# Moving reciprocals, seeds and a transpose in the attention stage of a fused attention and SoLU kernel

## The chip, the cores and the metric

The kernel runs on one core of a Trainium2 chip. The metric is the device time of one execution in microseconds; the figure for a kernel is the median of its runs. Five engines work side by side, each through its own instructions in the order in which the program gives them: PE (TensorE, the matmuls), DVE (VectorE), ACT (ScalarE), POOL (GpSimd) and SP (SyncE, which here issues nearly all DMAs). They wait for one another and for DMAs through semaphores.

## The reference

The kernel computes attention with normalised queries and keys, and feeds its output into a feed-forward block.

```python
# q, k, v: (8, 12, 448, 64)
q_n, k_n = rmsnorm(q, g_q), rmsnorm(k, g_k)     # x / sqrt(mean(x*x) + 1e-6) * g
attn = softmax(q_n @ k_n.T / 8)                 # rows of 448
x = (attn @ v), heads side by side              # (3584, 768)
h = x @ w_in                                    # (3584, 1024)
solu = h * softmax(h)
ln = (solu - mean) / sqrt(var + 1e-6) * g_ln
out = ln @ w_out                                # (3584, 768)
```

The softmax of the attention is not divided out where it is computed. The exponentials go into the value product as they are; their row sums are computed beside, are inverted, and are multiplied in later, when `x` is read for the product with `w_in`.

## The kernel before, in words

All of the work lies in `fast_path`. It has three stages one after the other: attention, the product with `w_in` with the SoLU and its normalisation, and the product with `w_out`. Both products are by a scheme with seven block products in place of eight. The order of the instructions is written out by hand (`tc.manual_schedule()`), so the order of the lines in the loop is the order on each engine.

**Attention by quads.** The 96 pairs of batch and head are taken four at a time, which makes 24 quads (`NQ`). The loop over `m` from 1 to 23 does one quad in each turn. A turn works on several quads at once:

- PE computes the scores of quad `m` in seven pieces of 64 keys (`both_scores`, L885) and the products with the values (`both_values`, L897). ACT takes the exponential of each piece (`exponentials`, L845). The output of the values lies in one PSUM buffer, `o`, of which there is one only: before PE may begin the values of quad `m`, DVE must have copied out the quad before (`take(m - 1)`, L1000, `xo<-o`).
- DVE adds up the exponentials of the quad so that the row sums need fewer matmuls: `add_pair` (L905), `add_to` (L911) and, for the quads in the table `two_terms`, `join_terms` (L915), which adds the two partial sums `es` into one. What is left are the quad's terms: the exponentials `El` of the last piece, and one or two `es`. After each quad in `sums_at` (2, 5, 8, 11, ..., 23) PE sums the terms of the quads since the last such place with matmuls against ones (`sums`, L962, eight matmul records for each term), ACT copies the result (L974), and SP sends it to DRAM (`sd`, L979).
- For quad `m + 1`, POOL scales queries and keys by their inverse norms (`normalise`, L735, `qkn`), DVE transposes the two halves (`qk_transpose`, L756, `qkT`), and ACT multiplies the gain in (`gains`, L751). The scores of quad `m + 1` wait for that.
- For quad `m + 2` the norms are prepared: ACT squares (L690), DVE sums rows (`row_sums`, L696), POOL folds the sums (`fold_sums`, L706 and L707), ACT makes a first guess of the inverse root by a logarithm and an exponential (`rsqrt_seed`, L713 and L714) and, if told to, its square (L717). At the start of the next turn DVE improves the guess (`rsqrt_step`): where the square is there by L724 and L729, otherwise by L727, L728 and L729.
- For 12 turns (`steps_at`) ACT and DVE also convert a piece of `w_in` (L538, L539 on ACT, L545 and L546 on DVE), and POOL combines blocks of `w_in` (`combine_in`, L567) after a gate (L570).

**The inverses.** The table `inverts_at` says in which turn the row sums of a batch are inverted: turns 4, 8, 10, 14, 16, 20 and 22. At the start of such a turn SP loads them from DRAM (`load_sums`, L988, `inv<-sd`). At the end of the turn, behind the additions and before `take(m)` of the next turn, DVE takes the reciprocal (`invert`, L992). In the turn after, SP writes them back (`send_inverses`, L995).

**SP's queue.** In each turn SP issues, in this order: the values of quad `m + 1` (`load_v`, L675), the output of the last quad (`store_x`, L1009, which waits for `take(m - 1)`), the sums and inverses if there are any (L979, L995, L988), a piece of `w_in` (L513), and eight to ten pieces of queries and keys of a later quad (L647). One instruction that waits holds up all that stand behind it.

Of the kernel before, what the change touches and what calls it, by code (L numbers as in the profile page):

```python
# [366 lines left out]
def fast_path(  # L367
# [24 lines left out]
    nc = tc.nc  # L392
# [294 lines left out]
    def squares(n):  # L687
        d = st[n]
        d["sq"] = work.tile([P, 2 * NB, 32], FP32, tag="sq", name="sq", bufs=2)
        nc.scalar.activation(d["sq"].rearrange("p (s b) d -> p s (b d)", s=2), d["qk"], AF.Square)  # L690

    def row_sums(n):
        m, i = divmod(n, 2)
        if i == 0:
            norms[m] = {"part": work.tile([P, 2, 2 * NB], FP32, tag="part", name="part", bufs=2)}
        nc.vector.tensor_reduce(norms[m]["part"][:, i], st[n]["sq"], AX, OP.add)  # L696
# [12 lines left out]
    def rsqrt_seed(d, square=False):  # L709
        ss = d["ss"]  # L710
        p, w = ss.shape
        y = d["y"] = work.tile([P, 4 * NB], FP32, tag="ny", name="ny", bufs=2)[0:p, 0:w]
        nc.scalar.activation(y, ss, AF.Ln, scale=1.0 / D, bias=eps[0:p])  # L713
        nc.scalar.activation(y, y, AF.Exp, scale=-0.5)  # L714
        if square:
            x = d["x"] = work.tile([P, 4 * NB], FP32, tag="nx", name="nx", bufs=2)[0:p, 0:w]
            nc.scalar.activation(x, y, AF.Square)  # L717
# [35 lines left out]
    def qk_transpose(n):  # L753
        d = st[n]
        turned(n)
        nc.vector.transpose(d["qkT"].rearrange("p s t -> p (s t)"), d["qkn"].rearrange("p b d -> p (b d)"))  # L756
# [709 lines left out]
    combines_at = {11 + 3 * (x // 2) + x % 2: (x,) for x in range(8)}  # L1466
    combines_at[22] = (8,)
    combines_at[23] = (10, 11)
    two_terms = (3, 4, 6, 7, 9, 10, 12, 13, 15, 16, 18, 19, 21, 22, 23)
    sums_at = (2, 5) + tuple(range(8, NQ, 3))  # L1470
    inverts_at = {4: (0,), 8: (1,), 10: (2,), 14: (3,), 16: (4,), 20: (5,), 22: (6,)}
    wq += [(moe_w_out, c + k, i) for c in range(HF) for k in (0, HF) for i in range(2)]
# [31 lines left out]
    with tc.manual_schedule():  # L1504
# [68 lines left out]
        for m in range(1, NQ):  # L1573
            a, b = 2 * m, 2 * m + 1
            next1 = m + 1 < NQ
            next2 = m + 2 < NQ
            early = EARLY <= m
            four = m < 3

            def score(x):  # L1580
                unit(lambda: both_scores(m, x))

            def value(x):
                unit(lambda: both_values(m, x))

            if m == 3:
                norm_gain()
            sent = None
            if kept:
                sent = keep_sums(*kept)  # L1590
                kept = None
            if next1:
                load_v(m + 1)
            beside = combines_at.get(m, ())
            if beside:
                if m - 1 in steps_at:
                    step = wq[steps_at.index(m - 1)]
                    pass_on(w_in[(0, 3, 1, 2)[step[1] // HD * 2 + step[2]]][0:1, step[1] % HD, 0:1])
                else:
                    pass_on(quads[m - 1]["terms"][-1][1][0:1, 0, 0:1])  # L1600
                for x in beside:
                    combine_in(x)
                take(m - 1)
            if early and next1:
                rsqrt_step(norms[m + 1])
            if m > 1 and not beside:
                take(m - 1)
            store_x(m - 1)
            if sent:
                sent()  # L1610
            for x in inverts_at.get(m - 1, ()):
                send_inverses(x)
            for x in inverts_at.get(m, ()):
                load_sums(x)
            if early and m + 2 in steps_at:
                load_next()
            if m == 1:
                score(0)
                score(1)
                score(2)  # L1620
                rsqrt_seed(norms[2])
                rsqrt_step(norms[2])
                normalise(4)
                normalise(5)
                load_pieces(8)
                score(3)
                squares(6)
                row_sums(6)
                qk_transpose(4)
                value(0)  # L1630
                score(4)
                squares(7)
                row_sums(7)
                qk_transpose(5)
                value(1)
                score(5)
                fold_sums(3)
                value(2)
                score(6)
                gains(2)  # L1640
                rsqrt_seed(norms[3])
                add_pair(m, 0, 1)
                add_to(m, 0, 2, nc.vector)
            else:
                if next1:
                    if not early:
                        rsqrt_step(norms[m + 1])
                    if m == 2:
                        add_pair(1, 3, 4)
                        quads[1]["terms"].append((2, quads[1]["E", 5]))  # L1650
                    normalise(a + 2)
                    normalise(b + 2)
                    if m == 22:
                        combine_in(9)
                if early:
                    load_pieces(2)
                else:
                    load_pieces(10)
                    if m + 2 in steps_at:
                        load_next()  # L1660
                if early and next2:
                    row_sums(a + 4)
                    row_sums(b + 4)
                    load_pieces(6)
                if m == NQ - 1:
                    scale(0)
                score(0)
                if m > 2 and not early:
                    squares(a + 4)
                    row_sums(a + 4)  # L1670
                score(1)
                if next1:
                    qk_transpose(a + 2)
                if m > 2 and not early:
                    squares(b + 4)
                    row_sums(b + 4)
                if m == 2:
                    score(2)
                    squares(a + 4)
                    row_sums(a + 4)  # L1680
                    score(3)
                    squares(b + 4)
                    row_sums(b + 4)
                    qk_transpose(b + 2)
                else:
                    if next1:
                        qk_transpose(b + 2)
                    score(2)
                    score(3)
                if next2:  # L1690
                    fold_sums(m + 2)
                value(0)
                score(4)
                if m in steps_at:
                    low_bits, join, product = convert_w(wq[steps_at.index(m)], raws[steps_at.index(m)])
                    low_bits[0]()
                value(1)
                score(5)
                if m in steps_at:
                    low_bits[1]()  # L1700
                if next1 and early and m not in sums_at:
                    gains(m + 1)
                add_pair(m, 0, 1)
                if four:
                    add_to(m, 0, 2, nc.vector)
                    add_pair(m, 3, 4)
                else:
                    add_pair(m, 2, 3)
                    add_to(m, 0, 4, nc.vector)
                    add_to(m, 1, 5, nc.vector)  # L1710
                    if m in two_terms:
                        join_terms(m)
                value(2)
                score(6)
                if next1 and (not early or m in sums_at):
                    gains(m + 1)
                if m in steps_at:
                    join()
                if next2:
                    rsqrt_seed(norms[m + 2], True)  # L1720
                if m + 1 >= EARLY and m + 3 < NQ:
                    squares(a + 6)
                    squares(b + 6)
                if four:
                    quads[m]["terms"].append((2, quads[m]["E", 5]))
            quads[m]["terms"].insert(0, (2, quads[m]["E", NK - 1]))
            if m == NQ - 2:
                load_x(0)
                load_r(0)
            if m == NQ - 1:  # L1730
                load_x(1)
                sizes(0)
                block_sums(0, 0)
                block_sums(0, 1)
            for x in inverts_at.get(m, ()):
                invert(x)
            for x in range(3, NK):
                value(x)
            waiting.append(m)
            if m in sums_at:  # L1740
                unit(lambda: None)
                kept = end_sums()
                waiting.clear()
# [188 lines left out]
```

## Time and profile before

| what | value |
|---|---|
| median of 3 runs | 780.86 us (780.45 to 781.51) |
| the profiled execution's own time | 782.57 us |
| its span from first to last instruction | 780.8 us |
| PE busy | 767.3 us (98%) |
| DVE busy | 612.4 us (78%) |
| ACT busy | 514.1 us (66%) |
| POOL busy | 486.6 us (62%) |

The page gives the busy time of each engine, in forty slices of the span too, the chain of work that ended last, and groups of instructions by line. Attention takes the stretch up to about 298.7 us, where the first matmul with `w_in` (L1114) begins; from 548.7 us on the last of these are under way, and the products with `w_out` (L1340) follow. A row of the timeline gives start, duration, engine, line, operation, what is written from what is read, and how often; in square brackets stands how long the engine was idle ahead of it, and who ended that.

### The profile page before, as it was taken

What the parts mean: (1) busy time and instruction counts of PE and PEld (TensorE: products, weight loads), DVE (VectorE), ACT (ScalarE), POOL (GpSimd) and SP (SyncE); (2) the same over time, 40 slices, a digit from 0 to 9 for tenths busy, and PEclk for the clock granted to TensorE, in tenths of its full rate; (3) what the DMA queues carried; (4) which work ended last, traced back from release to release, by engine and by line L of the source; (5) the groups of instructions that cost most, each with busy time, mean ns of one, the idle gap of its engine ahead of it and who ended that gap; (6) DMA issues with size and microseconds to landing.
All of it is one profiled execution on the core that took longest, in us unless ns stands there. A gap on an engine that the chain in (4) does not pass through costs nothing.

```text
span 780.8 us, 14823 instructions
## 1 busy us (share of the span) xinstructions
PE 767.3 (98%) x5142; PEld 473.8 (61%) x5142; DVE 612.4 (78%) x1034; ACT 514.1 (66%) x853; POOL 486.6 (62%) x635
## 2 busy tenths in 40 slices
PE   8999999999999999999999999999999999999996
PEld 4444444444444444444444444444899999999996
DVE  6779999999999984687878766685797685776844
ACT  6688898988989862787777756655626445464410
POOL 2554543455464452455677688888898787777852
PEclk9999999999999999999999999999999999999999
DMA  9999999999999376588887767773756647446212
GB/s 159 169 188 178 206 166 201 200 189 182 209 196 183 104 180 143 142 197 182 199 187 179 165 148 166 166 179 70 224 157 232 209 143 256 155 176 247 98 62 86
DMA packets 279817, 134.26 MB, mean 172 GB/s; under 512 B 190324, under 2 KB 264884, under 8 KB 279732
## 3 DMA queue, kind: packets, MB, share of 16 engines
q1 hardware_dynamic: 265892, 123.31, 70.5%
q10 hardware_dynamic: 13840, 9.90, 4.3%
q8 instruction: 43, 0.70, 0.4%
q14 instruction: 42, 0.34, 0.1%
HBM read 96.12 MB, written 37.04 MB: 171 GB/s over the span
## 4 chain that ended last, share of the span: by engine, by line
PE 83%; SPq 6%; DVE 4%; DMA 3%; issue 2%; POOL 2%; ACT 1%; DVEq 0%; POOLq 0%; ACTq 0%
PE A L1340 16%; PE A L1114 14%; PE s L885 10%; PE o L897 10%; PE B L1114 9%; PE B L1340 8%; PE D L1114 5%; PE C L1114 5%; SPq L647 4%; PE C L1340 4%; PE sm L962 2%; POOL qkn L735 1%; DMA qk<-in_q_dram 1%; DVE es L911 1%; DMA qk<-in_k_dram 1%
## 5 line engine op out<-in xcount | busy, mean ns | idle before, releaser
L885 PE MATMUL s<-qkT 64*64 64x448 f32 x1288 | 140.5, 542 | 1.1 <-ACT qkT L751 1.0
L845 ACT ACTIVATE E<-s 128x896 f32<-128x896 f32 x144 | 124.4, 920 | 18.5 <-PE s L885 17.8
L897 PE MATMUL o<-E,v 64*64 64x448 f32 x1104 | 120.8, 537 | 1.6 <-DVE xo L1000 1.1
L735 POOL TENSOR_TENSOR qkn<-qk,ny 128x896 f32<-128x896 f32 x45 | 77.2, 1736 | 67.7 <-DVE ny L729 32.4
L885 PEld LDWEIGHTS s<-qkT 64*64 64x64 f32 x1288 | 66.2, 191 | 61.9 <-issue 37.9
L1340 PE MATMUL A<-w_out,sums 128*128 128x192 f32 x392 | 79.7, 326 | 0.0
L1340 PE MATMUL B<-w_out,sums 128*128 128x192 f32 x392 | 79.7, 326 | 0.0
L897 PEld LDWEIGHTS o<-E,v 64*64 64x64 f32 x1104 | 42.0, 133 | 58.9 <-issue 47.9
L1114 PE MATMUL A<-w_in,xg 128*128 128x512 f32 x168 | 76.8, 593 | 0.0
L1114 PE MATMUL B<-w_in,xsum 128*128 128x512 f32 x168 | 76.7, 592 | 0.0
L1340 PEld LDWEIGHTS A<-w_out,sums 128*128 128x128 f32 x392 | 66.3, 190 | 0.0
L1340 PEld LDWEIGHTS B<-w_out,sums 128*128 128x128 f32 x392 | 66.3, 190 | 0.0
L756 DVE STREAM_TRANSPOSE qkT<-qkn 128x896 f32<-128x896 f32 x46 | 50.0, 1099 | 9.7 <-POOL qkn L735 9.7
L1114 PEld LDWEIGHTS B<-w_in,xsum 128*128 128x128 f32 x168 | 31.9, 190 | 40.2 <-issue 39.9
L1114 PEld LDWEIGHTS A<-w_in,xg 128*128 128x128 f32 x168 | 31.8, 190 | 40.1 <-issue 38.9
L1216 ACT ACTIVATE u<-u,shift,he 128x1024 f32<-128x1024 f32 x28 | 34.8, 1242 | 28.7 <-POOL shift L1212 28.6
L696 DVE TENSOR_REDUCE part<-sq 128x28 f32<-128x896 f32 x46 | 47.9, 1075 | 6.3 <-ACT sq L690 6.3
L1090 POOL TENSOR_TENSOR xsum<-xg 128x384 f32<-128x384 f32 x14 | 14.4, 1032 | 57.9 <-ACT xsum L1073 45.1
L905 DVE TENSOR_TENSOR es<-E 128x896 f32<-128x896 f32 x46 | 49.4, 1110 | 0.0
L911 DVE TENSOR_TENSOR es<-es,E 128x896 f32<-128x896 f32 x44 | 47.9, 1126 | 0.1
L1340 PE MATMUL A<-w_out,s 128*128 128x192 f32 x224 | 45.5, 326 | 0.0
L690 ACT ACTIVATE sq<-qk 128x896 f32<-128x896 f32 x45 | 41.0, 945 | 3.2 <-DMA qk<-in_k_dram 2.4
(175 smaller groups left out, 1660.7 us busy)
## 6 DMA issues: line engine op xcount, KB each, us to landing
ur<-ud SPq DMA_DIRECT2D x60, 256.0 KB, 4.6
ud<-ub SPq DMA_DIRECT2D x112, 128.0 KB, 2.9
xd<-xo SPq DMA_DIRECT2D x48, 224.0 KB, 4.1
qk<-in_q_dram SPq DMA_DIRECT2D x92, 112.0 KB, 4.5
qk<-in_k_dram SPq DMA_DIRECT2D x92, 112.0 KB, 4.2
v<-in_v_dram SPq DMA_DIRECT2D x23, 448.0 KB, 3.9
out_dram<-P SPq DMA_DIRECT2D x19, 384.0 KB, 4.0
raw<-in_moe_w_in_dram SPq DMA_DIRECT2D x12, 512.0 KB, 5.7
```

Of the source, the lines that this page charges most:

```text
L690: nc.scalar.activation(d["sq"].rearrange("p (s b) d -> p s (b d)", s=2), d["qk"], AF.Square)
L696: nc.vector.tensor_reduce(norms[m]["part"][:, i], st[n]["sq"], AX, OP.add)
L735: e.tensor_tensor(d["qkn"].rearrange("p (s b) d -> p s b d", s=2), d["qk"].rearrange("p s (b d) -> p s b d", d=32), y.rearrange("p (s b) - ...
L756: nc.vector.transpose(d["qkT"].rearrange("p s t -> p (s t)"), d["qkn"].rearrange("p b d -> p (b d)"))
L845: nc.scalar.activation(e, s[:, :, 0:S], AF.Exp)
L885: nc.tensor.matmul(s[i * D : (i + 1) * D, h, 0:S], qkT[hh, i, 1, keys], qkT[hh, i, 0], start=True, stop=True)
L897: nc.tensor.matmul(d["o"][h * D : (h + 1) * D, i, 0:S], d["v"][pp, h, kc], d["E", kc][pp, h], start=kc == 0, stop=kc == NK - 1,)
L905: nc.vector.tensor_tensor(e, d["E", x], d["E", y], OP.add)
L911: engine.tensor_tensor(e, e, d["E", x], OP.add)
L1114: nc.tensor.matmul(k[bank], a[:, c], w_in[i][:, c], start=begin and c == 0, stop=c == HD - 1, skip_group_check=not begin,)
L1216: nc.scalar.activation(d["u"], d["u"], AF.Identity, scale=d["e"], bias=d["shift"])
L1340: nc.tensor.matmul(k[bank], a[:, c].rearrange("p a i -> p (a i)"), w_out[:, area, i, c], start=begin and c == 0, stop=c == KC - 1, skip_gr ...
```

## The change

The change makes five edits, all in the loop over the quads, and no other function is touched.

1. `invert(x)` moves, for the turns from 4 on, from the end of the turn to the place right behind the second `qk_transpose`, ahead of the additions. `load_sums` and `send_inverses` stay where they are.
2. In turn 1 the second transpose comes ahead of `row_sums(7)`; the seed for quad 3 and two additions of quad 1 move from the end of turn 1 into turn 2. There the additions are first, then `score(0)`, then the seed.
3. Quads 21 and 23 leave the table `two_terms`: they keep two `es` and El, three terms.
4. The square of the seed by ACT is left out in turns 6, 9, 12, 15, 18 and 21; in the turn that follows, DVE does `rsqrt_step` with three instructions in place of two.
5. The first entry of a quad's terms is put in with `setdefault`, since quad 1 has no terms yet at that place.

```diff
-    two_terms = (3, 4, 6, 7, 9, 10, 12, 13, 15, 16, 18, 19, 21, 22, 23)
+    two_terms = (3, 4, 6, 7, 9, 10, 12, 13, 15, 16, 18, 19, 22)
...
+                qk_transpose(5)
                 row_sums(7)
-                qk_transpose(5)
...
-                rsqrt_seed(norms[3])
-                add_pair(m, 0, 1)
-                add_to(m, 0, 2, nc.vector)
             else:
+                if m == 2:
+                    add_pair(1, 0, 1)
+                    add_to(1, 1, 2, nc.vector)
+                    score(0)
+                    rsqrt_seed(norms[3])
...
-                score(0)
+                if m != 2:
+                    score(0)
...
                     if next1:
                         qk_transpose(b + 2)
+                    for x in inverts_at.get(m, ()):
+                        invert(x)
                     score(2)
                     score(3)
...
-                    rsqrt_seed(norms[m + 2], True)
+                    rsqrt_seed(norms[m + 2], m not in steps_at or m + 1 in steps_at)
...
-            quads[m]["terms"].insert(0, (2, quads[m]["E", NK - 1]))
+            quads[m].setdefault("terms", []).insert(0, (2, quads[m]["E", NK - 1]))
...
-            for x in inverts_at.get(m, ()):
-                invert(x)
```

On DVE the rows of turn 8 show the first edit (`qkT` is the transposed queries and keys, `inv` the row sums to be inverted, `es` the added exponentials, `w_in_90` a block of weights):

```order
 L696 TENSOR_REDUCE part<-sq 128x28 x2
 L756 STREAM_TRANSPOSE qkT<-qkn 128x896 x2
+L992 RECIPROCAL inv<-inv 128x42
 L905 TENSOR_TENSOR es<-E 128x896 x2
 L911 TENSOR_TENSOR es<-es,E 128x896 x2
 L545 SCALAR_TENSOR_TENSOR tmp<-raw,tmp 128x512
 L546 SCALAR_TENSOR_TENSOR w_in_90<-raw,tmp 128x512
-L992 RECIPROCAL inv<-inv 128x42
```

The reciprocal moved ahead of four additions and of the two steps of a weight's conversion; nothing else in the turn moved.

On DVE the rows from the end of turn 1 into turn 2 show the second edit (`part` are the row sums of squares, `xo` the copy of a quad's output):

```order
 L696 TENSOR_REDUCE part<-sq 128x28
-L756 STREAM_TRANSPOSE qkT<-qkn 128x896
+L756 STREAM_TRANSPOSE qkT<-qkn 128x896 x2
 L696 TENSOR_REDUCE part<-sq 128x28
-L756 STREAM_TRANSPOSE qkT<-qkn 128x896
+L1000 COPY xo<-o 128x896
 L905 TENSOR_TENSOR es<-E 128x896
 L911 TENSOR_TENSOR es<-es,E 128x896
-L1000 COPY xo<-o 128x896
```

The second transpose moved one place up, ahead of the row sums, and the copy of the output moved ahead of two additions.

On PE the rows at the end of attention show the third edit (`sm` are the row sums in PSUM, `El` the exponentials of the last piece, four matmuls of the program for each term, in the order of quads 21, 22 and 23):

```order
 L962 MATMUL sm<-El,ones 32x224 x4
+L962 MATMUL sm<-es,ones 32x224 x8
+L962 MATMUL sm<-El,ones 32x224 x4
 L962 MATMUL sm<-es,ones 32x224 x4
 L962 MATMUL sm<-El,ones 32x224 x4
-L962 MATMUL sm<-es,ones 32x224 x4
-L962 MATMUL sm<-El,ones 32x224 x4
-L962 MATMUL sm<-es,ones 32x224 x4
+L962 MATMUL sm<-es,ones 32x224 x8
 L1114 MATMUL A<-w_in_88,xg 128x512 x3
```

There are two more groups of four matmuls with `es`: one for quad 21 and one for quad 23, the latter last of all.

## Prediction

> **What bounds the kernel now.** I read the page first, then PE's waits, then busy times by stage, then the timelines of DVE, PE and SP at the places where the change acts.
>
> ```profile
> PE 767.3 (98%) x5142; PEld 473.8 (61%) x5142; DVE 612.4 (78%) x1034; ACT 514.1 (66%) x853; POOL 486.6 (62%) x635
> ```
>
> PE is the engine that sets the time: from the first scores to the last product it hardly rests. So an edit gains only where PE waits today, and costs only where it makes PE wait. PE's waits that the change can touch:
>
> ```profile
> PE sm L962 <- DVE es L915: 1.4, 1, 1.4
> PE o L897 <- DVE xo L1000: 1.1, 2, 0.6
> PE s L885 <- ACT qkT L751: 1.0, 1, 1.0
> ```
>
> These are 3.5 us in all. More telling are the busy times in attention (columns: stretch, its length, busy time and instructions of PE, PEld, DVE, ACT, POOL, then clock, DMA share, GB/s):
>
> ```profile
> 80.00:120.00 40.00, 40.00 (x456) 18.83 (x452) 39.72 (x48) 36.40 (x55) 17.19 (x27) 1.00 0.98 188
> 160.00:200.00 40.00, 40.00 (x452) 19.36 (x448) 38.38 (x45) 36.03 (x52) 20.84 (x31) 1.00 1.02 200
> ```
>
> PE is full, but DVE is too, at 96 to 99%, and so are the DMA engines, with a share of about 1. The 78% of DVE on the page is a mean over three stages and hides that. DVE has no lead over PE either, at the end of attention (DVE's copy of quad 21's output; PE's first value product of quads 22 and 23):
>
> ```profile
> 274.02 1.08 DVE L1000 COPY xo<-o 128x896 f32<-128x896 f32 x1
> ```
>
> ```profile
> 275.15 0.98 PE L897 MATMUL o<-E,v 64*64 64x448 f32 x8
> 286.96 0.98 PE L897 MATMUL o<-E,v 64*64 64x448 f32 x8 [0.57 <-DVE xo L1000]
> ```
>
> The copy ends at 275.10 and PE begins 0.05 us later; one quad on, PE waits 0.57. So whatever DVE loses anywhere in attention has become PE's loss by quad 23. That is the reading on which the rest hangs.
>
> **The reciprocals (edit 1).** The instruction costs the same at either place. What counts is when its input lands. In turn 8 DVE does this:
>
> ```profile
> 113.22 2.10 DVE L756 STREAM_TRANSPOSE qkT<-qkn 128x896 f32<-128x896 f32 x2
> 115.23 2.05 DVE L905 TENSOR_TENSOR es<-E 128x896 f32<-128x896 f32 x2
> 117.20 2.09 DVE L911 TENSOR_TENSOR es<-es,E 128x896 f32<-128x896 f32 x2
> 119.93 0.69 DVE L546 SCALAR_TENSOR_TENSOR w_in<-raw,tmp 128x512 uint32<-128x512 uint32 x1
> 120.99 0.42 DVE L992 RECIPROCAL inv<-inv 128x42 f32<-128x42 f32 x1 [0.37 <-DMA qk<-in_q_dram]
> 121.33 0.15 DVE L724 SCALAR_TENSOR_TENSOR nx<-ss,nx 128x56 f32<-128x56 f32 x1
> ```
>
> SP issued the load here:
>
> ```profile
> 115.80 1.23 SPq L1009 DMA_DIRECT2D xd<-xo  x2
> 117.09 0.84 SPq L988 DMA_DIRECT2D inv<-sd  x1
> ```
>
> The reciprocal waited even at its late place: 0.37 us, for a DMA. Its input landed at 120.99, 3.9 us after the issue. In the new place DVE comes to it at 115.23, when the load is not yet issued, and stands for 5.8 us. Behind it on DVE are the four additions, the two weight steps, the norm's step and the copy `xo`; for these wait PE's sums, POOL's `qkn`, PE's values and SP's store. The additions begin at 121.33 instead of 115.23, 6.10 later. From the step of the norm on (121.33 before) the delay is 6.10 less what is vacated between 120.62, when L546 ends, and 121.33: 5.39.
>
> PE feels it first at the sums of turn 8, whose last two terms are this quad's `es`:
>
> ```profile
> 121.33 0.94 PE L962 MATMUL sm<-es,ones 128*32 128x224 f32 x16
> ```
>
> The last addition ends 6.10 after 119.29 (117.20, where L911 starts, and its 2.09), at 125.4. PE begins the second of the two terms 0.38 us (the step between two terms, below) behind 121.33, at 121.7, so it loses 3.7 there; the rest of the 5.39 comes as DVE's lead goes over the next quads.
>
> Would the early gain of edit 2 (below, 1.0) be kept? Only as far as SP comes earlier, since the landing sets the time here. SP goes from one issue to the next (117.03, 117.09) on DMA engines that are full, so it can hardly come earlier by all of that; I count about two thirds, 0.65, as earlier landing: 5.39 - 0.65 = 4.74.
>
> For the other turns SP's lag no longer holds: when DVE is 5 us later, SP has caught up and is held by the copy `xo` itself. Turn 4 shows that spacing (DVE's copy, then SP), and a tile's answer for turn 16 the landing:
>
> ```profile
> 63.97 1.08 DVE L1000 COPY xo<-o 128x896 f32<-128x896 f32 x1
> ...
> 69.24 1.10 DVE L756 STREAM_TRANSPOSE qkT<-qkn 128x896 f32<-128x896 f32 x1
> ```
>
> ```profile
> 65.08 1.26 SPq L1009 DMA_DIRECT2D xd<-xo  x2
> 66.40 1.58 SPq L988 DMA_DIRECT2D inv<-sd  x1
> ```
>
> ```profile
> DMA to landing us min/median/max: 3.5/3.5/3.5
> ```
>
> So the inverse lands 1.35 + 3.5 = 4.85 us after the copy ends. Turns 10 and 14 show how long DVE takes from the copy's end to the end of the transposes:
>
> ```profile
> 133.46 1.08 DVE L1000 COPY xo<-o 128x896 f32<-128x896 f32 x1
> 136.45 2.10 DVE L756 STREAM_TRANSPOSE qkT<-qkn 128x896 f32<-128x896 f32 x2
> ```
>
> ```profile
> 178.78 1.08 DVE L1000 COPY xo<-o 128x896 f32<-128x896 f32 x1
> 184.14 1.11 DVE L756 STREAM_TRANSPOSE qkT<-qkn 128x896 f32<-128x896 f32 x1 [0.46 <-POOL qkn L735]
> ```
>
> That is 4.0 us in turn 10, where the norm's step comes ahead of the copy, 5.4 in turn 14 and 5.3 in turn 4. Turn 16 has the order of turn 10, turns 20 and 22 that of 14. I count 1.0 each for turns 10 and 16, and nothing for 4, 14, 20 and 22, where the transposes cover the load by about 0.5. If SP still lagged in 14 and 20, each would add up to about 1; that goes into the range.
>
> [...]
>
> **The squares (edit 4).**
>
> ```profile
> L717 ACT ACTIVATE nx<-ny x20: 249/249/251, 49.6 to 271.6; 128x56 f32<-128x56 f32 x20
> L728 DVE TENSOR_TENSOR nx<-nx,ny x5: 174/216/218, 6.9 to 39.5; 128x56 f32<-128x56 f32 x3, 112x16 f32<-112x16 f32 x2
> ```
>
> ACT sheds six of these, 1.5 us, and it is nobody's bound there. DVE gains six at 0.22. The one in turn 7 is swallowed by the wait in turn 8; the other five add 1.1 to a full engine. In turns 10, 13, 16 and 19 it stands ahead of the copy, in turn 22 ahead of POOL's `qkn`.
>
> **Three terms (edit 3).** The join of quad 21 takes 1.09 us of DVE, just ahead of quad 22's copy: -1.09. At the end of attention (DVE's adds and join of quad 23; PE's sums):
>
> ```profile
> 271.68 1.09 DVE L915 TENSOR_TENSOR es<-es 128x896 f32<-128x896 f32 x1
> ```
>
> ```profile
> 292.62 3.70 DVE L911 TENSOR_TENSOR es<-es,E 128x896 f32<-128x896 f32 x2
> 296.35 1.77 DVE L915 TENSOR_TENSOR es<-es 128x896 f32<-128x896 f32 x1
> ```
>
> ```profile
> 295.80 0.56 PE L962 MATMUL sm<-es,ones 128*32 128x224 f32 x8
> 296.18 0.56 PE L962 MATMUL sm<-El,ones 128*32 128x224 f32 x8
> 298.18 0.59 PE L962 MATMUL sm<-es,ones 128*32 128x224 f32 x8 [1.44 <-DVE es L915]
> ```
>
> Without the join, quad 23's second `es` is ready at 296.32 instead of 298.12. PE spends 0.38 us on a term (295.80 to 296.18) and has two more, 0.76; it comes to the last one later than 296.32 and doesn't wait. So the end gets 1.44 - 0.76 = 0.68 shorter.
>
> **The third quad (edit 2).** PE waits ahead of the scores of quad 2:
>
> ```profile
> 37.35 3.69 PE L885 MATMUL s<-qkT 64*64 64x448 f32 x32 [0.96 <-ACT qkT L751]
> ```
>
> ```profile
> 34.16 1.04 DVE L696 TENSOR_REDUCE part<-sq 128x28 f32<-128x896 f32 x1
> 35.12 1.10 DVE L756 STREAM_TRANSPOSE qkT<-qkn 128x896 f32<-128x896 f32 x1
> ```
>
> With the row sums behind the transpose, that ends 0.96 earlier, and the 0.96 goes. The seed then waits for a POOL that gets its sums about 1 us later, but stands behind the first exponential and no longer holds it. I take the gain as 1.0, with 0 and 1.4 as its bounds; the wait in turn 8 swallows most of it in any case, as counted above. Edit 5 moves nothing.
>
> **The sum.** DVE at quad 22's copy: 4.74 + 2.0 (turns 10, 16) + 1.1 (steps) - 1.09 (join) = 6.75 later. The end: 6.75 - 0.68 = 6.1. The two later stages are PE without a gap, and shift as a whole. The profiled execution took 782.57 us, with its span of 780.8 inside; the median is 780.86, 1.7 below it. Forecast: 782.57 + 6.1 = 788.7 for that execution, 787.0 for the median.
>
> Its own bounds: 785.3 if SP comes earlier by the whole early gain and turns 10 and 16 cost half; 789.7 if SP comes no earlier and turns 14 and 20 cost 1 each.
>
> PE will stand still for some 3.7 us in turn 8, longer than any wait of before after its start. [...]
>
> **The rivals.**
>
> *The inverses are there in time: faster.* If SP came 5.8 us earlier in turn 8, or at any rate ahead of the transposes, no reciprocal would wait. Then the gains stand alone: 0.96 at quad 2, 0.57 at quad 23's copy (the join of quad 21 gives DVE 1.09, the added steps take 1.1, the start gives 0.96) and 0.68 at the end, 2.2 in all: 778.6. It decides at a landing before 115.23. For it: the load's time hangs on a DMA backlog that another order can shift. Against it: 5.8 us is half a turn, and compute that comes 1 us earlier makes SP's lag larger, not smaller. Chance 0.08.
>
> *SP stays behind in every turn.* If the lag is fixed against DVE and not against the clock, each turn pays its own. The load of turn 10:
>
> ```profile
> 139.51 0.73 SPq L988 DMA_DIRECT2D inv<-sd  x1
> ```
>
> With 3.5 to 3.9 us to landing, turn 10 would wait from 138.5 until about 143.2, 4.7 us. If turns 14, 16 and 20 are no better, that is 18.8 in place of 2.0: up to 804. Against it: SP gets 5 us of rest in which the DMAs drain. Chance 0.07.
>
> *The wait is absorbed.* DVE's delay of turn 8 could be made up if it has more lead than the rows show, or the load may land so much sooner that only 1 to 2 us are left against the gains: 780 to 782. The two rows leave DVE 0.3 and 1.6 us in 40, and those rests are waits for POOL such as the 0.46 in turn 14, which come along. Chance 0.08 for within 0.2%.
>
> **How the numbers follow.** The forecast has 0.76. It and the second rival are slower: 0.83; faster 0.09, same 0.08 (0.2% is 1.6 us, about what a measurement of this kernel can tell from none). The range, 782.3 to 792.5, takes the forecast's own bounds, reaches down to the absorbed wait and up to one or two turns that wait as the second rival has it.
>
> **What would show it.** Right: in turn 8 DVE idle for 5 to 6 us ahead of L992, ended by a DMA; a wait of PE of 3 to 4 us for `es` at the sums of turn 8; about 1 us ahead of L992 in turns 10 and 16; no wait ahead of the last sums; the first L1114 at about 304.8 instead of 298.7. Wrong: L992 without a wait in turn 8, or the first L1114 below 299.

## The result and the profile after

The changed kernel takes 790.94 us (median of 4 runs, 790.05 to 792.71), the kernel before, run beside it, 781.00: a ratio of 1.013, with an interval of 1.0111 to 1.0149. The change costs 9.9 us; 787.0 was forecast. The profiled execution took 791.04 us with a span of 789.4, so the two spans differ by 8.6. The rest of the 9.9 comes from the two profiled executions: that of before (782.57 us) was itself longer than its median, that of after was not.

The page's first line, then two of PE's waits:

```profile
PE 769.7 (97%) x5158; PEld 473.1 (60%) x5158; DVE 610.2 (77%) x1038; ACT 511.8 (65%) x847; POOL 483.3 (61%) x635
```

```profile
PE o L897 <- DVE xo L1000: 6.4, 8, 1.5
PE sm L962 <- DVE es L911: 2.9, 5, 1.2
```

PE's waits for DVE's copy `xo` went from 1.1 to 6.4 us, and a wait for the additions is new. DVE's waits name the place:

```profile
DVE inv L992 <- DMA inv<-sd: 8.6, 5, 3.7
```

The reciprocal stands for its load in five turns, 8.6 us in all; before, that was 0.37. The busy times by stage show whom it costs (columns as in the prediction):

```profile
80.00:120.00 40.00, 40.00 (x468) 18.94 (x464) 36.05 (x45) 36.44 (x53) 16.50 (x26) 1.00 1.05 191
...
160.00:200.00 40.00, 38.08 (x428) 17.82 (x424) 36.88 (x45) 33.67 (x49) 19.25 (x27) 1.00 0.98 179
```

In the stretch up to 120 us DVE now rests (36.05 us busy instead of 39.72), and in the later stretch PE does (38.08 instead of 40.00). The clock column stays at 1.00. Turn 8 on DVE, on SP and on PE:

```profile
112.47 2.10 DVE L756 STREAM_TRANSPOSE qkT<-qkn 128x896 f32<-128x896 f32 x2
118.24 0.42 DVE L992 RECIPROCAL inv<-inv 128x42 f32<-128x42 f32 x1 [3.68 <-DMA inv<-sd]
118.57 2.02 DVE L905 TENSOR_TENSOR es<-E 128x896 f32<-128x896 f32 x2
120.52 2.08 DVE L911 TENSOR_TENSOR es<-es,E 128x896 f32<-128x896 f32 x2
```

```profile
112.19 2.41 SPq L1009 DMA_DIRECT2D xd<-xo  x2
114.65 0.69 SPq L988 DMA_DIRECT2D inv<-sd  x1
```

```profile
121.65 0.59 PE L962 MATMUL sm<-es,ones 128*32 128x224 f32 x8 [1.22 <-DVE es L911]
122.66 0.59 PE L962 MATMUL sm<-es,ones 128*32 128x224 f32 x8 [0.41 <-DVE es L911]
```

The mechanism is the forecast's, a size smaller: in turn 8 DVE stands for 3.68 us instead of 5 to 6, and PE for 1.63 (1.22 and 0.41) instead of 3.7. SP issued the load at 114.65, 2.44 earlier than in the trace of before. The rest of the loss came in other turns. In two of them, 10 and 14, DVE and SP do this:

```profile
136.29 1.08 DVE L1000 COPY xo<-o 128x896 f32<-128x896 f32 x1
...
142.40 0.42 DVE L992 RECIPROCAL inv<-inv 128x42 f32<-128x42 f32 x1 [1.03 <-DMA inv<-sd]
...
183.26 1.08 DVE L1000 COPY xo<-o 128x896 f32<-128x896 f32 x1
...
191.62 0.42 DVE L992 RECIPROCAL inv<-inv 128x42 f32<-128x42 f32 x1 [1.89 <-DMA inv<-sd]
```

```profile
137.40 1.27 SPq L1009 DMA_DIRECT2D xd<-xo  x2
138.72 0.68 SPq L988 DMA_DIRECT2D inv<-sd  x1
...
186.28 1.24 SPq L1009 DMA_DIRECT2D xd<-xo  x2
187.57 0.68 SPq L988 DMA_DIRECT2D inv<-sd  x1
```

In turn 10 SP stores `xo` 0.03 us after the copy ends (137.37), in turn 14 it comes 1.94 after it (184.34): SP is behind again. Turn 16 waits 0.76 and turn 20 1.25.

The first matmul with `w_in` begins at 306.55 instead of 298.69, and no wait stands ahead of the last sums any more:

```profile
305.30 0.56 PE L962 MATMUL sm<-El,ones 128*32 128x224 f32 x8
305.68 0.94 PE L962 MATMUL sm<-es,ones 128*32 128x224 f32 x16
306.55 1.13 PE L1114 MATMUL A<-w_in,xg 128*128 128x512 f32 x2
```

DVE's copy of quad 22's output ends at 295.65 instead of 286.91, 8.74 later, and the first matmul is 7.86 later. That is most of the 8.6. The other 0.8 us lies behind the last matmul. The program's last line, in the kernel after (engine, how often, shortest, median and longest duration in ns, first and last start in us):

```profile
L1930 DVEq EVENT_SEMAPHORE  x2: 21/21/21, 787.5 to 788.0; - x2
L1930 PEldq EVENT_SEMAPHORE  x2: 51/51/51, 787.5 to 789.4; - x2
```

and in the kernel before:

```profile
L1927 DVEq EVENT_SEMAPHORE  x2: 21/21/21, 780.2 to 780.7; - x2
L1927 PEldq EVENT_SEMAPHORE  x2: 51/51/51, 780.2 to 780.7; - x2
```

PE's last semaphore instruction comes 1.4 us after DVE's; before, both came together.

### The profile page after: what moved, and what is told of

It reads as the page before. It is cut to its first block, busy times and chain, and to the rows that moved or that the text cites. A ratio compares the mean times of both kernels' runs of the same rounds, so it can differ in the third digit from the quotient of the medians.

```text
span 789.4 us, 14850 instructions
## 1 busy us (share of the span) xinstructions
PE 769.7 (97%) x5158; PEld 473.1 (60%) x5158; DVE 610.2 (77%) x1038; ACT 511.8 (65%) x847; POOL 483.3 (61%) x635
## 4 chain that ended last, share of the span: by engine, by line
PE 72%; DVE 10%; SPq 5%; issue 5%; DMA 4%; POOL 3%; ACT 1%; DVEq 0%
PE A L1340 16%; PE A L1114 14%; PE B L1114 9%; PE B L1340 8%; PE D L1114 5%; PE C L1114 5%; PE o L897 4%; PE C L1340 4%; SPq L647 4%; PE s L885 4%; POOL qkn L735 3%; DVE xo L1000 2%; DVE es L905 2%; DVE qkT L756 2%; DVE es L911 2%
## 5 line engine op out<-in xcount | busy, mean ns | idle before, releaser
L885 PE MATMUL s<-qkT 64*64 64x448 f32 x1288 | 138.8, 540 | 0.0
L1114 PE MATMUL A<-w_in,xg 128*128 128x512 f32 x168 | 76.8, 593 | 0.0
L1114 PE MATMUL B<-w_in,xsum 128*128 128x512 f32 x168 | 76.7, 592 | 0.0
L1114 PEld LDWEIGHTS B<-w_in,xsum 128*128 128x128 f32 x168 | 31.9, 190 | 40.2 <-issue 39.7
L1114 PEld LDWEIGHTS A<-w_in,xg 128*128 128x128 f32 x168 | 31.8, 190 | 40.1 <-issue 38.9
```

The source lines that it names most:

```text
L885: nc.tensor.matmul(s[i * D : (i + 1) * D, h, 0:S], qkT[hh, i, 1, keys], qkT[hh, i, 0], start=True, stop=True)
L1114: nc.tensor.matmul(k[bank], a[:, c], w_in[i][:, c], start=begin and c == 0, stop=c == HD - 1, skip_group_check=not begin,)
```

## The experiments

Theory A, the forecast's: the reciprocal at its new place stands for a load that SP issues too late, and all that is queued behind it on DVE is late. Rival B: the loss lies elsewhere (the order of quads 2 and 5, the squares, the three terms), and the place of the reciprocals matters little. The times of the kernel before, in the runs beside these, have medians of 781.1 to 781.6.

**The reciprocals at their old place, all else as changed.**

```diff
-                    for x in inverts_at.get(m, ()):
-                        invert(x)
...
+            for x in inverts_at.get(m, ()):
+                invert(x)
```

> The changed kernel with its reciprocals back at the end of the turn (edits 2 to 5 alone). Theory A, the waits for the landing of the inverses make the loss: the 8.6 us of waits ahead of the reciprocals go, and so does about 1.1 us that the copies and norm steps behind them lost to POOL; the early and the last wait of PE stay away: 779.5 us, between 778.5 and 780.5, a little faster than before (781.0). Rival B, the three-instruction steps and the moved additions load DVE so that it falls behind: 785 to 791 us, and the first matmul with w_in later than 301 us.

Measured: 781.58 us, ratio 1.0003 (0.9993 to 1.0012). The whole loss is gone, so rival B falls. But no gain is left either, where A had expected 1.6 us. What PE waits for DVE's copies (before: 1.1):

```profile
PE o L897 <- DVE xo L1000: 2.3, 4, 0.7
```

Attention ends 1.1 us earlier than before (first L1114 at 297.59), but the way from the last matmul with `w_out` to the end is 7.35 us instead of 6.17.

**The reciprocals at the new place, nothing else changed.**

```diff
+                    for x in inverts_at.get(m, ()):
+                        invert(x)
...
-            for x in inverts_at.get(m, ()):
-                invert(x)
```

> The kernel before with edit 1 alone. Theory A: waits ahead of the reciprocal in turns 8, 10, 14, 16 and 20 of 8 to 11 us together, 790 to 793 us. Rival B: reciprocals cost nothing by themselves, 781 to 783 us.

Measured: 792.14 us, ratio 1.0152 (1.0129 to 1.0174): 11.0 us between the medians for the move alone.

```profile
DVE inv L992 <- DMA inv<-sd: 9.7, 5, 3.9
```

In the profiles attention ends 10.1 us later than before (first L1114 at 308.83). The waits ahead of L992 give 9.3 of that (9.7, against 0.37 before). What is left, 0.8, is about the size of one more effect, which the groups by line show. L724, the first step of the norm, in the kernel before:

```profile
L724 DVE SCALAR_TENSOR_TENSOR nx<-ss,nx 128x56 f32<-128x56 f32 x20 | 6.8, 340 | 0.0
```

and here:

```profile
L724 DVE SCALAR_TENSOR_TENSOR nx<-ss,nx 128x56 f32<-128x56 f32 x20 | 7.9, 397 | 0.0
```

The same 20 instructions take 1.1 us longer. In the changed kernel, 14 of them take 6.3 us, and 5.2 with the reciprocals back at the old place. Turn 11 of the kernel after, on DVE and on POOL, shows how:

```profile
147.80 1.08 DVE L1000 COPY xo<-o 128x896 f32<-128x896 f32 x1
148.80 0.63 DVE L724 SCALAR_TENSOR_TENSOR nx<-ss,nx 128x56 f32<-128x56 f32 x1
```

```profile
148.09 1.27 POOL L567 TENSOR_TENSOR w_in<-w_in,w_in 128x512 f32<-128x512 f32 x1
```

L724 ends at 149.43, just after POOL's addition, at 149.36. The same rows of before:

```profile
143.56 0.41 DVE L992 RECIPROCAL inv<-inv 128x42 f32<-128x42 f32 x1
143.89 1.05 DVE L1000 COPY xo<-o 128x896 f32<-128x896 f32 x1
144.86 0.34 DVE L724 SCALAR_TENSOR_TENSOR nx<-ss,nx 128x56 f32<-128x56 f32 x1
```

```profile
143.85 1.27 POOL L567 TENSOR_TENSOR w_in<-w_in,w_in 128x512 f32<-128x512 f32 x1
```

Here the two end at 145.20 and 145.12, but with the reciprocal ahead of the copy L724 begins 1.01 us after POOL, and not 0.71. The 0.3 us of the reciprocal had cost nothing in that place, if L724 could not end before POOL in any case. That L724 follows POOL's end is read from the rows; no run took POOL's addition away.

**The loads of turns 8, 14 and 20 a turn earlier.**

```diff
+    loads_at = {4: (0,), 7: (1,), 10: (2,), 13: (3,), 16: (4,), 19: (5,), 22: (6,)}
...
-            for x in inverts_at.get(m, ()):
+            for x in loads_at.get(m, ()):
                 load_sums(x)
```

> The changed kernel, with the loads of the row sums for turns 8, 14 and 20 issued one turn earlier, so that they have landed when DVE comes to the reciprocal there; turns 10 and 16 cannot have it, their sums are sent only one turn ahead. Theory A: the waits of 3.7, 1.9 and 1.2 us in turns 8, 14 and 20 go and those of about 1 us in 10 and 16 stay: 784 us, between 783 and 786. If the loss came from the reciprocal's place and not from its load (rival B): 789 to 791 us.

Measured: 788.49 us, ratio 1.009 (1.0074 to 1.0107); much less is won than expected. The waits in turns 8, 14 and 20 are gone, but turn 10 stands for 4.84 us and turn 16 for 1.53, so that the waits only fall from 8.6 to 6.4 us in all:

```profile
133.02 1.08 DVE L1000 COPY xo<-o 128x896 f32<-128x896 f32 x1
...
142.93 0.42 DVE L992 RECIPROCAL inv<-inv 128x42 f32<-128x42 f32 x1 [4.84 <-DMA inv<-sd]
```

```profile
137.94 1.27 SPq L1009 DMA_DIRECT2D xd<-xo  x2
139.26 0.79 SPq L988 DMA_DIRECT2D inv<-sd  x1
```

DVE is 3.3 us earlier in turn 10 than in the changed kernel, and the load still lands at 142.93 (142.40 there). SP comes to the store 3.84 us after the copy has ended (3.65 in the kernel before, where DVE did not wait for it): it works off its queue at its own rate, and an earlier DVE waits longer. So the wait of turn 8 had covered that of turn 10. The prediction's second rival had named 4.7 us for this turn; the mechanism is right where nothing ahead of it waits.

The long stop also shows in the clock. PE in turn 11, then the busy times of that stretch:

```profile
149.48 1.77 PE L897 MATMUL o<-E,v 64*64 64x448 f32 x8 [3.77 <-DVE xo L1000]
151.02 1.71 PE L885 MATMUL s<-qkT 64*64 64x448 f32 x8
152.52 0.97 PE L897 MATMUL o<-E,v 64*64 64x448 f32 x8
153.32 0.92 PE L885 MATMUL s<-qkT 64*64 64x448 f32 x8
154.07 0.93 PE L897 MATMUL o<-E,v 64*64 64x448 f32 x8
```

```profile
149.40:152.50 3.10, 3.02 (x16) 1.04 (x20) 3.07 (x6) 0.00 (x0) 2.69 (x3) 0.50 1.19 172
152.50:155.60 3.10, 3.10 (x40) 1.47 (x36) 2.64 (x3) 2.79 (x4) 2.83 (x6) 0.98 0.82 268
```

After 3.77 us without work the granted clock is 0.50 for 3.1 us: 16 matmuls take 3.04 us (149.48 to 152.52), the next 16 take 1.55 (to 154.07). That is 1.5 us lost on PE. At the end of attention nothing of it is left: the first matmul with `w_in` (304.66) and DVE's copy of quad 22 (293.76) both come 1.89 us ahead of the changed kernel's, so it was DVE that set the time. In the attention of the changed kernel PE's longest wait was 1.5 us, and the clock stayed at 1.00.

**The reciprocal a turn after its load.** It still stands between the transposes and the additions, and the write-back comes a turn later.

```diff
-        inverses[b] = small.tile([P, H * S // P], FP32, tag="inv", name="inv", bufs=1)
+        inverses[b] = small.tile([P, H * S // P], FP32, tag="inv", name="inv", bufs=2)
...
-            for x in inverts_at.get(m - 1, ()):
+            for x in inverts_at.get(m - 2, ()):
                 send_inverses(x)
...
-                    for x in inverts_at.get(m, ()):
+                    for x in inverts_at.get(m - 1, ()):
                         invert(x)
...
+        send_inverses(6)
```

> The changed kernel with the reciprocals still between transposes and additions, but one turn after the load of their row sums, and the write back one turn later too (two buffers for the row sums). Theory A: no reciprocal waits, so 780 to 781 us, 1 us above the kernel with the reciprocals at the end of the turn since the copies behind the additions still meet POOL. Rival B: 788 us or more.

Measured: 782.06 us, ratio 1.001 (1.0 to 1.0019), and no wait ahead of L992. That is above the 780 to 781 expected, but far below rival B's 788. The place between transposes and additions does little harm by itself: L724 behind POOL is still there (14 of them take 6.1 us, and 5.2 with the old place), and the time is 0.5 us above that of the old place, with overlapping intervals. By far the most of the 9.9 us is the load's lateness. With the run of the old place this settles theory A.

The next eight kernels ask where the gains of the other edits went, and what holds PE's last semaphore instruction. All of them have the reciprocals at the old place.

**Two terms again in quads 21 and 23** (the table `two_terms` of before, the rest as in the first experiment).

> The changed kernel with the reciprocals back at the ends of their turns and quads 21 and 23 summed as two terms again, so that only the edits to quads 2 and 5 and to the squares are left. Theory: the three-term sums bring the attention's end about 0.7 us forward, but the 16 more PE records that they bring make PE's last semaphore come 1.3 to 1.9 us after those of the other engines, so that they cost more than they give. Then the last w_out matmul comes about 0.7 us later than in the kernel with the reciprocals at their old place (774.3 instead of 773.6), the way from it to the last instruction falls from 7.35 to 5.7 to 6.2 us, and the time is 780.5 to 781. Rival: the late semaphore belongs to something else in the change, the way to the end stays at 7.3 us and the time is 782.3.

Measured: 782.31 us, ratio 1.0013 (1.0004 to 1.0022). PE's last semaphore comes with DVE's again (way to the end 5.64 us), as the theory had it. Its price does not hold: attention ends 1.0 later (298.58 against 297.59), and the kernel comes out 0.1%, or 0.8 us, above the first experiment's, not below it. The two intervals overlap, so that the three terms are worth more than the late semaphore costs is suggested here and not shown; the run of the three terms alone, below, points the same way.

**Three terms in quad 21 alone.**

```diff
-    two_terms = (3, 4, 6, 7, 9, 10, 12, 13, 15, 16, 18, 19, 22)
+    two_terms = (3, 4, 6, 7, 9, 10, 12, 13, 15, 16, 18, 19, 22, 23)
```

> As the kernel before this one, with three terms in quad 21 alone: 8 more PE records than before the change instead of 16. Theory: the gain of 1.09 us in VectorE's queue from quad 21's missing join is kept, and if the late semaphore grows with the records it is late by half (0.7 to 0.9 us: time 780.5 to 781), if it is a threshold it is late by all or by nothing (781.5 or 780). Rival: the late semaphore has nothing to do with the records; the way to the end is the same as in the run beside it and the time lower than there by up to 1 us.

Measured: 781.09 us, ratio 0.9996 (0.9987 to 1.0006), about 1 us more than the 780 that a semaphore in time was to give. The way to the end is 5.59 us, so the late semaphore goes by a threshold here: 16 more PE records have it (7.35 us), 8 have not.

**The three terms alone, on the kernel before.**

```diff
-    two_terms = (3, 4, 6, 7, 9, 10, 12, 13, 15, 16, 18, 19, 21, 22, 23)
+    two_terms = (3, 4, 6, 7, 9, 10, 12, 13, 15, 16, 18, 19, 22)
```

> The kernel before with three terms in quads 21 and 23 and nothing else of the change. Theory: the last w_out matmul ends 0.7 to 1.0 us earlier than in the kernel before (774.60), the way from it to the end rises from 6.17 to about 7.3 us, and the time is 781.1 to 781.6, no gain. Rival: the way to the end stays at 6.2 us and the whole gain is seen: 780.1 to 780.4.

Measured: 780.67 us, ratio 0.9989 (0.9979 to 0.9998), between the two expectations. PE's last semaphore is late here too, with 6.84 us from the last matmul to the end. The last matmul ends at 772.55 instead of 774.60, more than the edit accounts for. Up to quad 21 this kernel's instructions are those of before, and yet quad 2 begins at 36.67 instead of 37.35. SP's queue differs too:

```profile
114.71 0.59 SPq L988 DMA_DIRECT2D inv<-sd  x1
```

The load of turn 8 goes out at 114.71 here and at 117.09 in the trace of before: one execution of the same instructions differs from another by 2.4 us in SP's queue, though DVE is only 0.7 ahead there. Over the 13 profiled kernels that issue this load in turn 8, before and after among them, it lies between 114.49 and 117.09; the trace that the forecast stands on has the latest.

**Every square by ACT** (the edit to the squares undone; three terms and the order of quads 2 and 5 as changed).

```diff
-                    rsqrt_seed(norms[m + 2], m not in steps_at or m + 1 in steps_at)
+                    rsqrt_seed(norms[m + 2], True)
```

> The changed kernel with the reciprocals back at the ends of their turns and every square by ScalarE again, so that VectorE's steps have two instructions in all quads. Theory: VectorE sets the turns' length, and the 0.25 us that each three-instruction step added go: the attention ends 1.0 to 1.7 us earlier than in the kernel with the reciprocals at their old place, 780.0 to 780.6. Rival: the squares left ScalarE because its queue held the step up there; then ScalarE's work comes late and the time is the same, 781.6, or more.

Measured: 780.35 us, ratio 0.9987 (0.9978 to 0.9996), against 1.0003 with the squares as changed (the intervals just touch): 0.16%, 1.2 us, for that edit. Against the run before this one, which has not the order of quads 2 and 5 of the change, it is 0.02%: that order is worth nothing that shows in the time. In this trace SP is late again: the load of turn 8 goes out at 116.71, and the reciprocal, at its old place, waits 0.73 us.

**The squares by ACT, and three terms in quad 21 alone.**

> The parts of the change that have been worth something so far and no more: the order of quads 2 and 5, three terms in quad 21 alone, every square by ScalarE, the reciprocals at the ends of their turns. 8 more PE records than before the change. Theory (a threshold between 8 and 16 more records makes PE's last semaphore late): it comes with the other engines', the way from the last w_out matmul to the end is 5.6 us, and the time is about 0.5 us under that of the kernel with three terms in both quads: 779.6 to 780.0, ratio 0.998. Rival (the three terms of quad 23 are worth as much as the late semaphore costs): 780.3 to 780.5.

Measured: 780.39 us, ratio 0.9984 (0.9975 to 0.9993), with PE's last semaphore in time (5.68 us to the end). Against the kernel with three terms in both quads nothing is won that shows. The rival's time has come, and the traces fit it: attention ends 0.90 later (297.12 instead of 296.22), and the way to the end is 0.64 shorter.

**One, four and three matmuls in the warm-up.** These are the kernel with the squares by ACT and three terms in both quads, with fewer of the five matmuls at the start, whose result nobody uses.

```diff
-        for _ in range(5):
+        for _ in range(1):
             nc.tensor.matmul(o, w[:, 0:P], w, start=True, stop=True)
```

> The kernel with three terms in both quads, every square by ScalarE and the reciprocals at the ends of their turns, with one matmul in the warm-up at the start (L799) instead of five, so that it has 5150 PE records instead of 5158 and nothing near its end is changed. Theory that the number of PE's records makes its last semaphore late: it comes with those of the other engines (5.6 us behind the last w_out matmul instead of 6.32), the end is 0.7 to 1.3 us earlier and the time 779.0 to 779.7. Rival, that what was changed near the quads 21 and 23 does it: the way to the end stays at 6.3 to 7.6 us and the time at 780.35. Beside both: should the clock in the first 25 us fall below 1.00 without the warm-up, quad 2 begins later than at 35.9 us, and the time is longer by as much.

> The kernel with three terms in both quads, every square by ScalarE and the reciprocals at the ends of their turns, with four matmuls in the warm-up instead of five: 5156 PE matmul records. With the weight loads and PE's 186 semaphore instructions its trace should hold 10498 PE instructions. On time were 10470 and 10486, late were 10502. [...] Rival, that the delay grows with the records beyond some number: half as late as with 10502 (0.2 to 0.6 us).

> As the kernel before this one with three matmuls in the warm-up: 5154 PE matmul records, 10494 PE instructions. [...] PE then idles for about 2 us before the norm of the weights, less than the 3.65 us after which the kernel with one warm-up matmul began at half speed; if that holds, quad 1 begins at 25.0 to 25.6 us, and the time is about 0.7 us under that of the kernel with five: 779.4 to 779.9, the best so far. Rivals: the last semaphore still late (780.2 to 780.5); or a slow start as with one matmul (quad 1 at 28 us, time 781).

Measured: 781.12, 780.60 and 781.55 us, ratios 0.9993 (0.9984 to 1.0003), 0.9984 (0.9975 to 0.9992) and 0.9998 (0.9988 to 1.0007). In all three PE's last semaphore is in time. With four it stands so:

```profile
L1930 DVEq EVENT_SEMAPHORE  x2: 21/21/21, 778.5 to 779.0; - x2
L1930 PEldq EVENT_SEMAPHORE  x2: 51/51/51, 778.5 to 779.0; - x2
```

Matmuls left out at the very start cure an end that is 770 us away, so it goes with the number of PE instructions. It jumps between 10498 (in time) and 10502 (late; matmuls, weight loads and PE's 186 other instructions, as the trace counts them). The six profiled kernels with 10502 are late by 0.8 to 1.9 us, the eight with fewer by nothing. The rival for four warm-up matmuls, a delay of half the size, falls: with 10498 both semaphores come at 779.0. What in the number of instructions makes the last one late is not shown.

What is saved at the end is paid at the start. PE with one warm-up matmul, then with five:

```profile
6.88 0.23 PE L494 MATMUL pg<-ident,gg 1*128 1x1 f32 x1 [3.65 <-DVE gg L490]
...
10.57 4.76 PE L855 MATMUL s<-qkT 64*64 64x448 f32 x24 [0.62 <-ACT qkT L825]
```

```profile
10.38 2.52 PE L855 MATMUL s<-qkT 64*64 64x448 f32 x24 [0.77 <-ACT qkT L825]
```

After 3.65 us of rest the first 24 score matmuls take 4.76 us instead of 2.52. With four and with three they take 4.07 and 4.52, though the rests at the same place are 0 and 1.51. There the clock column falls; the stretches with four, then with three (columns as in the prediction):

```profile
10.00:13.20 3.20, 3.08 (x20) 1.08 (x24) 2.35 (x6) 1.44 (x4) 0.00 (x0) 0.50 1.29 196
```

```profile
8.00:14.80 6.80, 5.89 (x32) 2.70 (x32) 4.38 (x10) 3.72 (x7) 0.00 (x0) 0.50 0.97 169
```

The granted clock is 0.50 there. With one matmul the column reads 1.00 all through, from 10.50 to 15.20 too, although the same matmuls are as slow (4.76 us); why is not shown. Why the clock falls behind four matmuls, and not behind five with the same waits of 0.9 and 0.6 us after them (the kernel before), stays open. Quad 1 begins at 28.24, 26.51 and 27.51 us with one, four and three, and at 25.22 with five. The later start and the longer time that the run with one had named beside both theories have come (781.12 against 780.35), though not the clock below 1.00 that it named for them; the second rival of the run with three has come too.

## Why the prediction was right, and where it was not

The sign and the mechanism were right: the reciprocal waits for its load, the additions and the copy behind it are late, and DVE has no lead to cover it. The end of attention was forecast 6.1 later and came 7.86 later. Added up along DVE, at its copy of quad 22, 6.75 was forecast and 8.74 measured (measured: the waits in DVE's rows, and the steps from copy to copy on DVE, after against before):

| term | forecast | measured |
|---|---|---|
| turn 8, less the early gain | 4.74 | 2.58 |
| turns 10 and 16 | 2.0 | 1.03 + 0.76 |
| turns 14 and 20 | 0 | 1.89 + 1.25 |
| three-instruction steps | 1.1 | 1.2 |
| join of quad 21 | -1.09 | -1.09 |
| L724 behind POOL, turns 11, 15, 17, 21 | - | 1.1 |

- **Turn 8** was too dear. The step that failed is "it can hardly come earlier by all of that; I count about two thirds, 0.65": SP came 2.44 earlier. The kernel with the three terms alone shows that this is mostly no effect of the change: its issue lies there as well, at 114.71. That turn 8 cost less than forecast is therefore in good part chance. One trace gave the place of a busy queue to about 2.5 us, no better.
- **Turns 14 and 20** were counted at nothing; "SP has caught up and is held by the copy" is true of 10 and 16, where SP stores within 0.03 us of the copy's end, and not of 14, where SP is 1.94 behind. The bound "up to about 1" each was too low as well. The kernel with earlier loads shows why: SP keeps its own pace (its store in turn 10 comes 3.84 us after the copy there, 3.65 in the kernel before).
- **Turns 10 and 16**, the squares and the join came out as worked out; the run with every square by ACT gives 1.2 for the squares.
- **L724 behind POOL** was not foreseen. "The instruction costs the same at either place" is where it hides: if L724 could not end before POOL in any case, as the rows of turn 11 suggest (0.07 to 0.08 us behind POOL in both kernels), the 0.3 us of the reciprocal cost nothing at its old place in four turns.
- **The end**: -0.68 forecast, -0.88 measured (7.86 less 8.74), and no wait ahead of the last sums, as said. PE's late semaphore, 0.8 in the spans, was not foreseen.
- **The gain of quads 2 and 5** was said to be mostly swallowed by the wait in turn 8. Nothing of it shows in the time with the reciprocals at their old place either (0.9987 with it, 0.9989 without).
- **The clock**: PE did not stand still for 3.7 us in turn 8; no wait in attention was longer than 1.5 us, and the granted clock stayed at 1.00. In the kernel with earlier loads a wait of 3.77 was followed by 3.1 us at 0.50, which cost PE 1.5 us; at the end of attention nothing of it was left.
- **The landing** was about right: 3.9 and 3.5 us were counted, and the rows of turns 8, 10 and 14 have 3.6, 3.7 and 4.1 from the issue to the reciprocal. (For the 3.9 the trace of before names another load as what ended the wait; in the changed kernel's rows it names this one.)
- **One of the bounds**: 785.3 comes out with the early gain at 1.4, its own bound; with the 1.0 that the forecast took it is 785.6.
- **From the profile to the median**: 1.7 us were subtracted for both kernels. But the profiled execution of before was a long one and that of after was not (791.04 beside a median of 790.94). The forecast for the profiled execution, 788.7, was 2.3 us short; the other 1.6 of the 3.9 by which the forecast of the median fell short are this.

Among the rivals, the inverses in time and the absorbed wait did not come. Of SP's lag in every turn the changed kernel shows two turns (14 and 20), and the kernel with earlier loads shows the figure itself (4.84 against 4.7).

By parts, on the runs: the reciprocals cost 9.4 (790.94 less 781.58) to 11.0 us, the squares 1.2; the three terms bring 0.9, the order of quads 2 and 5 nothing that shows. The two best versions leave the reciprocals and the squares as they were; one has three terms in quad 21 alone, the other three terms in both quads and four warm-up matmuls. Both are 0.16% faster than before, inside the 0.2% that the prediction took as what a measurement can tell from none.

## What to carry to other kernels

Before an instruction that reads a DMA's result is moved ahead on a full in-order engine, compare the landing with the new place in each turn by itself, and take the place of a busy DMA queue from several executions: here it differed by 2.4 us between two traces of the same instructions, and by 2.6 over all. A wait that is removed can uncover a later one behind the same queue, so the price of a set of waits is not their sum: here 6.8 us were to go, and 2.2 went. An instruction's old place may have been free: look at what its neighbour waits for there.

## What the runs showed of the hardware

- The end moved with the number of PE instructions: with 10502 in the trace PE's last semaphore came 0.8 to 1.9 us after the other engines' (six kernels), with 10498 or fewer together with them (eight).
- After a stop of 3.77 us, in the kernel with earlier loads, PE ran for 3.1 us at a granted clock of 0.50; in the attention of the changed kernel, with waits of up to 1.5 us, the clock stayed at 1.00.
- A DVE step of two tensors (L724) that took 0.15 us at the end of turn 8 of before took 0.63 beside a POOL addition in turn 11 of after, and ended 0.07 us after it.
- With one, three or four matmuls of warm-up instead of five, the first 24 score matmuls took 4.07 to 4.76 us instead of 2.52. With four and three the granted clock was 0.50 for 3.2 and 6.8 us there; with one the clock column showed 1.00 and the matmuls were slow all the same.
- The same DMA, issued by SP among DMA engines that are busy to about 1.0, went out 2.4 us apart in two executions of the same instructions (114.71 and 117.09).
